# Sparse attention with a gated MLP: DRAM layout of w_in and strided keys, early buffers in w_out's room, and a planner with new DMA and SBUF-port models and newly searched keys

## The chip, the cores and the metric

One core of a Trainium2 chip runs the whole kernel. The metric is the device time of one execution in microseconds; the time before is the median of three runs. Engines: PE (TensorE, matmuls), DVE (VectorE), ACT (ScalarE), POOL (GpSimd), SP (SyncE, which here issues every DMA, in order, on one queue).

## The reference

Eight batches, eight heads, 576 positions, head size 64. Heads 0 to 3 attend to the last 32 positions, heads 4 to 7 to earlier positions of the same residue modulo 32. The result goes through a gated MLP with a spatial mix.

```python
scores = q @ k.T / 8            # masked: local band (h < 4) or strided (h >= 4)
attn = softmax(scores) @ v      # per head; x = heads side by side, (8, 576, 512)
h = relu(x @ w_in)              # w_in (512, 1024), float64
u, v = h[..., :512], h[..., 512:]
v_n = (v - mean(v)) / sqrt(var(v) + 1e-6)
v_s = w_spatial @ v_n + b_spatial          # over the 576 positions
out = (u * v_s) @ w_out         # w_out (512, 512), float64
```

## The kernel before, in words

The work is float32 on a PE that multiplies a rounded form, so each operand is split in a rounded part and a rest (`rnd`, L368, and `rest`, L382), and each product takes three matmuls (PROD, L65). A *unit* t is one batch and a pair of heads; units 0, 1 of a batch are local, 2, 3 strided (NHP = 4 a batch). A unit loads q, k and v, makes scores on PE (L468 local, L611 strided), softmax on DVE and ACT, transposes on DVE (L549, L665), spreads the transposed blocks by rounding copies (L378 on POOL, L376 on ACT), multiplies with v (L578, L681) and writes x, its rounded part by ACT (L398) and its rest by DVE (L386).

A batch then goes through `moe_1` (v tiles, L916: x by w_in's second half, with relu, mean and variance, `chain`, L870; then u, L958), `moe_tail` (the last 64 positions) and `moe_2` (spatial mix, L1038 with the tail's L1050 and L1051; gate, L1060; then the product with w_out by a scheme of seven block products, L1127, sums L1155, stores L1148).

The weights w_in and w_out are float64 in DRAM and are decoded on the core: for each block of 128 rows by 512 columns `words` (L732) loads 512 KB, ACT rescales the high word (L748), POOL or DVE takes three bits of the low word (L757), DVE merges them (L765); then `rnd` and `rest` split it. The first four blocks of w_in land in the vn buffer, the next in u and g buffers. w_out's blocks are combined (L784) and split into w_out_sb (L333).

Buffers are rings (`Ring`, `Buf`, L109 to L136): q, k and raw v have two each, and the third user waits for the first's readers. Unit 2's v lies in the xt buffer instead (L707). The strided keys go to two fixed halves of kbd (L339), by the parity of t, cleared once (L1249).

The order is not written out by hand. Every step is added to `Program` (L139) with a key (its priority), its choice of engines with a cost for each, and what it reads and writes. `order` (L177) plays a list schedule through: the engine that is free first takes the ready step with the lowest key, or hands it to another engine on which it would end sooner; the issue order of each engine is what comes out, and the chip then runs these fixed queues. KEYS (L40) holds the numbers: due keys `a` of the first eight units, keys of the weight blocks (`v`, `u`, `s`, `t`, `o`) and of their loads (`lv`, `lu`, `ls`, `lo`), fillers, and the offsets `p` and `b` of the product steps. The steps of batch 0 and later have keys from 0 to some 400, so a key below 0 goes ahead of them and one in the thousands behind. `dp` is a penalty on DVE: 4195 ns for steps that do not lock the port with POOL, -23103 ns (a preference) for those that do. A load is modelled by its bytes at 310 GB/s (L64, L405) with 2000 ns until others see it (L78). A step of DVE or POOL that uses the shared SBUF port waits in the model until the other's is over (`begin`, L194). `fillers` (L288) puts idle matmuls (L1308) into modelled gaps of PE.

Of the kernel before, what the change touches and what calls it, by code (L numbers as in the profile page):

```python
# [19 lines left out]
DM = H * D  # L20
DFF = 1024
HF = DFF // 2
P = 128
# [20 lines left out]
    "s": (10.2, 4874.8, -256.8, 6409.8,),  # L44
    "t": (-1208.4,),
    "o": (4940, 2540.1, 5013.1, -12547.9,),
    "cst": (-12548.1,),
    "lead": (-0.71,),
    "fill": (1087.1, -65.1, -84.5, -3603.9, -724.5, -3137.8,),
    "dp": (4195.2, -23103.3,),  # L50
    "dpt": (865.03,),
    "lv": (-1100.4, -14982.5, -8252.6, 965.3,),
    "lu": (-391.5, -714.9, 584.7, -450.2,),
    "lo": (-4609.9, -1286.9, 727, -106.8,),
    "ls": (3914.1, 2245.4, 3737.9, 8661.3, 3210,),
    "near": (1768.91,),
    "p": (8.97, 17.05, 0.39,),
    "b": (-3.32, -3.82, 4.52, -4.56, 6.06, 24.46, 13.81, 15.33, 0.17, -3.06, 18.98,),
# [5 lines left out]
DMA_RATE = 310.0  # L64
# [13 lines left out]
    DMA: dict.fromkeys(ENGINES, 2000.0),  # L78
# [20 lines left out]
class Fixed:  # L99
# [39 lines left out]
class Program:  # L139
# [3 lines left out]
    def __init__(self):  # L143
        self.ops, self.writer, self.readers, self.spare = [], {}, {}, {}
        self.tiled, self.port = {}, {}

    def add(self, key, choices, fn, reads=(), writes=(), spare=None, tiled=0, port=()):


        n = len(self.ops)  # L150
        if port:
            self.port[n] = port
        if spare is not None:
            self.spare[n] = spare
# [12 lines left out]
        for tok in (*reads, *writes):
            buf = tok[0]
            if isinstance(buf, Buf):
                deps.update(buf.before)  # L170
                if buf.n > buf.ring.bufs:
                    deps.update(buf.last.users[:1])
                buf.users.append(n)
        deps.discard(n)
        self.ops.append((key, choices, fn, deps))

    def order(self):  # L177
# [7 lines left out]
        free = dict.fromkeys(ENGINES, 0.0)  # L185
        wait = {e: [] for e in ENGINES}
# [4 lines left out]
        held_by = {DVE: (0.0, 0.0), POOL: (0.0, 0.0)}  # L191
# [23 lines left out]
        while len(issued) < len(ops):  # L215
# [39 lines left out]
            if e == PE:  # L255
# [4 lines left out]
            now = begin(n, e, max(free[e], ready_at[n][e]))  # L260
            locks = POOL in self.port.get(n, ())
            held = KEYS["dp"][locks] if now < KEYS["dpt"][0] * 1000.0 else 0.0
            other = [
                (begin(n, o, max(free[o] + queue(o, n), ready_at[n][o])) + c + held * (o == DVE), o)
                for o, c in ops[n][1]
                if o != e
            ]
            if other and min(other)[0] < now + cost + held * (e == DVE):
# [49 lines left out]
def attention_moe(ctx, tc, qT, kT, vl, vs, cst, eye, w_in, w_out, wsp, wtail, out):  # L318
# [14 lines left out]
    w_out_sb = sb.tile([P, len(BLOCKS), 2, 2, DM // 2], F32R, name="w_out_sb")  # L333
# [10 lines left out]

    r_q = Ring(sb, "q", [P, SP], F32, 2)
# [22 lines left out]
    def rnd(key, n, dst, src, reads, writes, engs=(ACT, DVE, POOL), blocks=False):  # L368

        cost = {ACT: 110 + 0.87 * n, DVE: 70 + 0.52 * n, POOL: 110 + 1.75 * n}  # L370
        if blocks:
            cost = {ACT: 200 + 0.85 * n, DVE: 175 + 0.5 * n, POOL: 175 + 0.9 * n}

        def fn(eng):
            if hasattr(eng, "activation"):
                eng.copy(dst(), src())  # L376
            else:
                eng.tensor_scalar(dst(), src(), 1.0, 0.0, op0=ALU.mult, op1=ALU.add)  # L378

        add(key, [(e, cost[e]) for e in engs], fn, reads, writes, port=(DVE,))  # L380
# [23 lines left out]
    def load(key, dst, src, writes, nbytes, reads=()):  # L404
        add(key, [(DMA, nbytes / DMA_RATE)], lambda eng: eng.dma_start(dst(), src), reads, writes)  # L405
# [10 lines left out]
    def normalise(key, st, m, n, p, dst, reads, writes):  # L416
# [12 lines left out]
            key, [(DVE, 70 + 1.04 * n * width), (POOL, 110 + 1.75 * n * width)],  # L429
# [163 lines left out]
    def strided_attention(t, due, q, k, v, vin, kin):  # L593
# [30 lines left out]
        if not masked:  # L624
# [16 lines left out]
            [(DVE, 70 + 1.04 * w)] + ([] if masked else [(POOL, 110 + 1.75 * w)]),  # L641
# [90 lines left out]
    def words(key, fetch, src, n, stage):  # L732
# [19 lines left out]
        def lowest(eng):  # L752
# [7 lines left out]
            key, [(DVE, 70 + 0.52 * n), (POOL, 110 + 1.8 * n)], lowest,  # L760
            [], [low], port=(DVE,),
# [11 lines left out]
    def parts(key, n, val, dst, reads, tok):  # L773
        rnd(key, n, lambda: dst(0), val, reads, [(*tok, 0)])
# [13 lines left out]
    def weight_blocks(kk, bufs):  # L788
# [21 lines left out]
        for b, (name, val, reads) in enumerate((  # L810
# [3 lines left out]
            parts(key, n, val, lambda j, b=b: w_out_sb[:, b, j, kk], reads, ("w_out", name, kk))  # L814
# [55 lines left out]
    def chain(key, v_ps, m, tok):  # L870
# [20 lines left out]
            key, [(POOL, 525)],  # L891
# [129 lines left out]
    def moe_2(b, key):  # L1021
# [98 lines left out]
        def product(block, name, o_ps, a, key, first):  # L1120
            buf, at = place[name]
            b_at = BLOCKS.index(block)
            for kk in range(2):

                def fn(eng, kk=kk):
                    for i, (w, j) in enumerate(PROD):
                        eng.matmul(  # L1127
                            o_ps()[:, :HS],
                            w_out_sb[:, b_at, w, kk, a * P : (a + 1) * P],
# [9 lines left out]
                     *(("w_out", block, kk, w) for w in range(2))],  # L1139
# [85 lines left out]
    add(KEYS["cst"][0], [(DMA, 330)], lambda eng: eng.dma_start(cst_sb, cst), (), [("cst",)])  # L1225
# [91 lines left out]
def _layout(q, k, v, w_in, w_spatial, b_spatial, w_out):  # L1317
# [11 lines left out]
    qT, kT = heads(q, SP, 0), heads(k, STRIDE + S, STRIDE)  # L1329
    vpad = np.zeros((nb, H // 2, S + 32, D), np.float32)  # L1330
# [17 lines left out]
    def words(w):  # L1348
# [11 lines left out]
        "kT": kT,  # L1360
# [4 lines left out]
        "w_in": words(w_in),  # L1365
# [25 lines left out]
```

## Time and profile before

| | |
|---|---|
| median of three runs | 522.7 us (522.42 to 523.24) |
| the profiled execution | 521.19 us |
| its span, first to last instruction | 519.2 us |
| granted PE clock over the span | 0.99 |
| moved by DMA | 52.65 MB, mean 101 GB/s |

The profile gives for each engine the time it was busy, by line and operation, what ended the idle time before it, and the chain of work that ended last. A busy PE is not a useful PE: matmuls overlap, and fillers count. Busy shares over the whole span are an average over a start that loads and decodes, a long even middle and an end, so windows of time are read one by one. SP is no computing engine: its rows are DMA issues, and a gap between two is a wait in its queue.

### The profile page before, as it was taken

How to read it: one execution, taken by the hardware profiler on the slowest of the kernel's cores; microseconds unless marked ns; L12 is line 12 of the kernel's file. 1: busy time of each engine (PE TensorE's matmuls, PEld its weight loads, DVE VectorE, ACT ScalarE, POOL GpSimd, SP SyncE). 2: the span in 40 equal slices, each digit the busy share in tenths (PEclk: the TensorE clock that was granted, in tenths of full speed). 3: DMA queues.
4: the chain of work that ended last, by engine and by line, in shares of the span. 5: the costliest groups of instructions: out<-in, count | busy, mean ns of one | idle time of the engine just before them, and what ended most of it. 6: DMA issues, size and time to landing. Idle time of an engine off the chain costs nothing.

```text
span 519.2 us, 14653 instructions
## 1 busy us (share of the span) xinstructions
PE 502.4 (97%) x5892; PEld 457.8 (88%) x5892; DVE 366.9 (71%) x1101; ACT 264.3 (51%) x809; POOL 125.0 (24%) x253
## 2 busy tenths in 40 slices
PE   7889899999999999999999999999999999999997
PEld 4568799889899899988998899998999899998996
DVE  2899999888597847967389655986469651776166
ACT  6768654678462576417645645534755342223221
POOL 3563542153230213202122212302204010101000
PEclk9799999999999999999999999999999999999999
DMA  7986433653033322252222502232112300020002
GB/s 242 323 293 217 144 135 107 200 179 107 31 115 123 108 73 67 102 156 80 72 95 84 176 1 79 88 122 75 41 55 64 111 0 2 2 89 4 1 1 91
DMA packets 26243, 52.65 MB, mean 101 GB/s; under 512 B 3136, under 2 KB 11584, under 8 KB 26176
## 3 DMA queue, kind: packets, MB, share of 16 engines
q1 hardware_dynamic: 26176, 51.72, 30.5%
q8 instruction: 46, 0.75, 0.6%
q14 instruction: 21, 0.17, 0.1%
HBM read 42.27 MB, written 9.44 MB: 100 GB/s over the span
## 4 chain that ended last, share of the span: by engine, by line
PE 71%; DVE 18%; ACT 4%; DMA 2%; POOL 2%; issue 2%; SPq 1%; DVEq 0%; POOLq 0%; ACTq 0%
PE m L958 18%; PE m L916 16%; PE m L1038 14%; PE m L1127 10%; DVE vn L386 3%; PE po L681 3%; PE po L578 3%; PE s L468 2%; DVE u L784 2%; PE s L611 1%; DVE g L386 1%; DVE u L1060 1%; PE m L1050 1%; PE m L1051 1%; DMA k<-kT 1%
## 5 line engine op out<-in xcount | busy, mean ns | idle before, releaser
L1038 PE MATMUL m<-wsp_sb,vn 128*128 128x288 f32 x768 | 113.5, 299 | 1.6 <-DVE wsp_sb L386 1.6
L1038 PEld LDWEIGHTS m<-wsp_sb,vn 128*128 128x128 f32 x768 | 106.8, 191 | 2.5 <-DVE wsp_sb L386 1.8
L958 PE MATMUL m<-x,w_in_sb 128*128 128x288 f32 x768 | 105.9, 297 | 0.0
L958 PEld LDWEIGHTS m<-x,w_in_sb 128*128 128x128 f32 x768 | 103.4, 188 | 1.4
L916 PE MATMUL m<-w_in_sb,x 128*128 128x512 f32 (+1 forms) x408 | 100.0, 398 | 0.4 <-DVE w_in_sb L386 0.2
L916 PEld LDWEIGHTS m<-w_in_sb,x 128*128 128x128 f32 (+1 forms) x408 | 74.0, 185 | 19.9 <-DVE x L386 0.9
L378 POOL TENSOR_SCALAR ptl<-pc 32x320 f32<-32x320 f32 (+3 forms) x104 | 40.3, 388 | 90.1 <-ACT x L398 32.3
L1127 PE MATMUL m<-g,w_out_sb 128*128 128x288 f32 x384 | 56.8, 299 | 0.2 <-ACT vv L398 0.2
L892 POOL TENSOR_TENSOR bn<-bn,sel 128x1 f32<-128x1 f32 (+1 forms) x37 | 21.4, 581 | 141.4 <-DVE bn L887 141.0
L386 DVE TENSOR_TENSOR x<-po,x 128x288 fp32r<-128x288 f32 x64 | 28.0, 450 | 37.3 <-ACT x L398 36.5
L1127 PEld LDWEIGHTS m<-g,w_out_sb 128*128 128x128 f32 x384 | 52.6, 188 | 1.1 <-ACT vv L398 0.4
L525 ACT ACTIVATE pl<-pl,ml 128x64 f32<-128x64 f32 (+1 forms) x140 | 46.9, 338 | 3.1 <-DVE ml L505 3.0
L874 ACT ACTIVATE vv<-m 128x512 f32<-128x512 f32 (+1 forms) x37 | 22.0, 594 | 47.6 <-PE m L916 41.2
L1127 PE MATMUL m<-vn,w_out_sb 128*128 128x288 f32 x288 | 44.0, 300 | 2.1 <-DVE vn L386 1.4
L1060 DVE TENSOR_TENSOR u<-m,u 128x288 f32<-128x288 f32 x64 | 28.0, 452 | 23.3 <-PE m L1051 22.9
L879 DVE BATCH_NORM_STATS2 bn<-vv 128x6 f32<-128x512 f32 (+1 forms) x37 | 25.4, 687 | 25.5 <-ACT vv L874 25.2
L1127 PEld LDWEIGHTS m<-vn,w_out_sb 128*128 128x128 f32 x288 | 39.6, 188 | 4.3 <-DVE vn L386 2.2
L398 ACT CAST x<-po 128x288 fp32r<-128x288 f32 x64 | 24.7, 398 | 36.0 <-PE po L578 24.3
L972 ACT ACTIVATE u<-m 128x288 f32<-128x288 f32 x64 | 25.9, 409 | 28.4 <-PE m L958 28.2
L376 ACT CAST g<-u 128x288 fp32r<-128x288 f32 x54 | 22.4, 432 | 27.1 <-DVE u L1060 20.6
L376 ACT COPY ptl<-pc 32x320 f32<-32x320 f32 (+3 forms) x88 | 31.4, 357 | 5.9 <-DVE pc L549 4.0
L899 DVE TENSOR_SCALAR vv<-vv,bn 128x512 f32<-128x512 f32 (+1 forms) x37 | 20.6, 557 | 19.3 <-POOL bn L892 19.1
(123 smaller groups left out, 726.5 us busy)
## 6 DMA issues: line engine op xcount, KB each, us to landing
q<-qT SPq DMA_DIRECT2D x32, 295.0 KB, 4.8
v_raw<-vs SPq DMA_DIRECT2D x15, 512.0 KB, 3.8
outT<-o SPq DMA_DIRECT2D x48, 144.0 KB, 1.9
v_raw<-vl SPq DMA_DIRECT2D x16, 384.0 KB, 3.4
k<-kT SPq DMA_DIRECT2D x16, 304.0 KB, 4.5
kbd<-kT SPq DMA_DIRECT2D x32, 144.0 KB, 4.2
outT<-vv SPq DMA_DIRECT2D x16, 144.0 KB, 3.1
vn<-w_in SPq DMA_DIRECT2D x4, 512.0 KB, 6.7
```

What stands on the lines that cost most here:

```text
L376: eng.copy(dst(), src())
L378: eng.tensor_scalar(dst(), src(), 1.0, 0.0, op0=ALU.mult, op1=ALU.add)
L386: eng.tensor_tensor(dst(), src(), f32(hi()), op=ALU.subtract)
L398: eng.copy(dst(), src())
L525: eng.activation(p_sb()[:m, u, :], src, AF.Exp, bias=st()[:m, u : u + 1], scale=SCALE if masked else -1.0, **total,)
L879: lambda eng: eng.bn_stats(bn()[:m, 0:6], v()[:m]), [(v,)], [(bn,)],
L916: eng.matmul(v_ps()[:m, :], x_at(kt)[:, a, :], w_in_sb[:, w, kt, HF:], start=(n == 0 and i == 0), stop=(n == NT - 1 and i == 2),)
L958: eng.matmul(u_ps()[:, :HS], w_in_sb[:, w, kt, f * P : (f + 1) * P], xs[NHP * b + kt]()[:, a, r], start=(n == 0 and i == 0), stop=(n == NT ...
L972: lambda eng, u=u, f=f, u_ps=u_ps: eng.activation(u()[:, f * HS : (f + 1) * HS], u_ps()[:, :HS], AF.Relu),
L1038: eng.matmul(s_ps()[:, :HS], vn()[:, a, kt, fs], wsp_sb[:, w, kt, r], start=(kt == 0 and i == 0), stop=False,)
L1060: lambda eng, ug=ug, s_ps=s_ps: eng.tensor_tensor(ug(), s_ps()[:, :HS], ug(), op=ALU.mult),
L1127: eng.matmul(o_ps()[:, :HS], w_out_sb[:, b_at, w, kk, a * P : (a + 1) * P], at(j, kk), start=first and kk == 0 and i == 0, stop=kk == 1 an ...
```

## The change

- **DRAM layouts.** The host stores w_in as blocks, so that a block's 128 rows of 512 columns lie in one run, and the strided heads' keys as `ks`, one run for each of the two loads of a unit.
- **Homes.** w_out_sb becomes the second user of a ring with one buffer; its first user, `room`, holds q of units 2 and 3 and v of unit 3 (`Part`). Unit 6's v joins unit 2's in xt. w_out's blocks are given keys no earlier than the dues of units 0 to 3, and wait for the readers of the room.
- **Planner: transfers.** A load occupies the queue for 470 ns, transfers stream one behind the other at 370 GB/s after a lag of 1500 ns, and are seen 500 ns after their last byte. ACT starts after a table load of 1280 ns.
- **Planner: port.** Two steps on the shared port run at the same time, each stretched by a share (`SLOWED`), and the stretch is handed on to those that wait.
- **Planner: costs.** New POOL costs for rounding, two-input steps (200 + 2.0n ns), the bit step and the power.
- **Keys.** All of KEYS is new, with `dp` at 12894.8 and -1038.4.

The arithmetic and the number of steps stay as they are.

```diff
 KEYS = {
-    "a": (-1571.4, -4625.4, -1560.3, -729.5, 1426.5, 1095.5, 1503.9, 1519,),
-    "v": (3216.4, -1871.4, 2555.7, -7289.2,),
-    "u": (3205.1, 9316, 1081.3, -773.8,),
+    "a": (-7906.0, -7964.0, -15830.5, -4267.6, 1379.5, 702.2, 2039.1, -3334.8,),
+    "v": (5971.0, -3908.5, -3534.4, 726.2,),
+    "u": (4329.4, -8322.8, -3410.6, -6121.6,),
...
-    "o": (4940, 2540.1, 5013.1, -12547.9,),
-    "cst": (-12548.1,),
+    "o": (1519.5, 3986.0, -8051.8, 12581.5,),
+    "cst": (-11921.6,),
...
-    "dp": (4195.2, -23103.3,),
+    "dp": (12894.8, -1038.4,),
...
-    "lv": (-1100.4, -14982.5, -8252.6, 965.3,),
-    "lu": (-391.5, -714.9, 584.7, -450.2,),
+    "lv": (-2858.0, -4582.1, -8989.4, -1041.3,),
+    "lu": (66.6, -1740.1, -5229.0, 1297.1,),
...
-    "p": (8.97, 17.05, 0.39,),
-    "b": (-3.32, -3.82, 4.52, -4.56, 6.06, 24.46, 13.81, 15.33, 0.17, -3.06, 18.98,),
+    "p": (2.79, 10.51, 0.21,),
+    "b": (25.62, -1.03, 29.44, -12.2, 10.78, 11.69, 33.63, 25.64, -64.18, 15.47, 14.89,),
 }
-DMA_RATE = 310.0
+SLOWED = ((0.3, 0.15), (0.45, 0.6), (0.9, 0.8))
+DMA_RATE, DMA_ISSUE, DMA_LAG, DMA_TAIL, TABLE_LOAD = 370.0, 470.0, 1500.0, 500.0, 1280.0
...
-        def begin(n, e, at):
+        def shared(n, e, at, cost):
             if e in self.port.get(n, ()):
-                since, until = held_by[peer[e]]
+                since, until, share, _ = held_by[peer[e]]
                 if since <= at < until:
-                    return until
-            return at
+                    both = min(until - at, cost)
+                    slow = SLOWED[max(share, self.share[n])]
+                    return (slow[0] * both, slow[1] * both) if e == DVE else (slow[1] * both, slow[0] * both)
+            return 0.0, 0.0
...
+            if e == DMA:
+                moved = max(moved, now + DMA_LAG) + self.bytes[n] / DMA_RATE
+                free[e] = max(now + DMA_ISSUE, moved - DMA_LAG)
+                end = moved + DMA_TAIL
...
-    w_out_sb = sb.tile([P, len(BLOCKS), 2, 2, DM // 2], F32R, name="w_out_sb")
+    r_wo = Ring(sb, "w_out_sb", [P, len(BLOCKS), 2, 2, DM // 2], F32R, 1)
+    room, w_out_sb = r_wo.new(), r_wo.new()
...
+    early_q = [part(NU * D + i * SP, SP) for i in range(2)]
+    early_v = Part(room, lambda t: part(0, NU * D).view(t).rearrange("p (u d) -> p u d", d=D))
...
-        cost = {ACT: 110 + 0.87 * n, DVE: 70 + 0.52 * n, POOL: 110 + 1.75 * n}
+        cost = {ACT: 110 + 0.87 * n, DVE: 70 + 0.52 * n, POOL: 200 + (1.65 if apart else 1.0) * n}
...
-        cost = {DVE: 70 + 1.04 * n + extra, POOL: 120 + 2.3 * n}
+        cost = {DVE: 70 + 1.04 * n + extra, POOL: 200 + 2.0 * n}
...
-        q, k = r_q.new(), None
-        if t == 2:
+        q, k = early_q[t - 2] if t in (2, 3) else r_q.new(), None
+        if t == 3:
+            v = place = early_v
+        elif t in (2, 6):
             place = r_xt.new()
...
-                    kT[b, hp, j::2, STRIDE:], [("k", t % 2, j)], 64 * S * 4, [("k0", t % 2)],
+                    ks[b, hp - 2, j], [("k", t % 2, j)], 64 * S * 4, [("k0", t % 2)],
...
-                    KEYS[name][i], KEYS["l" + name][i], w_in[rows, cols], HF,
+                    KEYS[name][i], KEYS["l" + name][i], w_in[i, c], HF,
...
-                max(KEYS["o"][kk], jobs[-1][0]) + 0.01 * kk,
+                max(KEYS["o"][kk], jobs[-1][0], *(due(t) for t in range(NHP))) + 0.01 * kk,
```

More of the change, by code (lines that the diff above doesn't have):

```diff
@@ L185, in order @@
         free = dict.fromkeys(ENGINES, 0.0)
+        free[ACT], moved = TABLE_LOAD, 0.0
         wait = {e: [] for e in ENGINES}
@@ L259, in order @@
                 cost += FETCH_COST * max(0.0, -stock)
-            now = begin(n, e, max(free[e], ready_at[n][e]))
-            locks = POOL in self.port.get(n, ())
+            now = max(free[e], ready_at[n][e])
+            locks = POOL in self.port.get(n, ()) and self.share[n] == 1
             held = KEYS["dp"][locks] if now < KEYS["dpt"][0] * 1000.0 else 0.0
[L263 to L268, printed above, removed]
+            other = []
+            for o, c in ops[n][1]:
+                if o != e:
+                    at = max(free[o] + queue(o, n), ready_at[n][o])
+                    other.append((at + c + shared(n, o, at, c)[0] + held * (o == DVE), o))
+            if other and min(other)[0] < now + cost + shared(n, e, now, cost)[0] + held * (e == DVE):
                 e = min(other)[1]
                 cost = dict(ops[n][1])[e]
-                now = begin(n, e, max(free[e], ready_at[n][e]))
+                now = max(free[e], ready_at[n][e])
             taken[n] = True
             if e in self.port.get(n, ()):
-                held_by[e] = (now, now + cost)
-            free[e] = now + cost
+                more, theirs = shared(n, e, now, cost)
+                cost += more
+                p = peer[e]
+                begun, until, share, m = held_by[p]
+                if theirs and free[p] == until:
+                    free[p] = until = until + theirs
+                    held_by[p] = (begun, until, share, m)
+                    for j in after[m]:
+                        for o in ENGINES:
+                            ready_at[j][o] = max(ready_at[j][o], until + LAT[p][o])
+                held_by[e] = (now, now + cost, self.share[n], n)
+            free[e] = end = now + cost
+            if e == DMA:
+                moved = max(moved, now + DMA_LAG) + self.bytes[n] / DMA_RATE
+                free[e] = max(now + DMA_ISSUE, moved - DMA_LAG)
+                end = moved + DMA_TAIL
             issued.append((now, n, e))
@@ L278, in order @@
                 for o in ENGINES:
-                    lag = LAT[e][o]
-                    ready_at[m][o] = max(ready_at[m][o], now + cost + lag)
+                    ready_at[m][o] = max(ready_at[m][o], end + LAT[e][o])
                 left[m] -= 1
@@ L317, in attention_moe @@
 @with_exitstack
-def attention_moe(ctx, tc, qT, kT, vl, vs, cst, eye, w_in, w_out, wsp, wtail, out):
+def attention_moe(ctx, tc, qT, kT, ks, vl, vs, cst, eye, w_in, w_out, wsp, wtail, out):
     nc = tc.nc
@@ L378, in fn @@
                 eng.tensor_scalar(dst(), src(), 1.0, 0.0, op0=ALU.mult, op1=ALU.add)
-        add(key, [(e, cost[e]) for e in engs], fn, reads, writes, port=(DVE,))
+        add(key, [(e, cost[e]) for e in engs], fn, reads, writes, port=(DVE, POOL), share=0)
     def rest(key, n, dst, src, hi, reads, writes, engs=(DVE, POOL), extra=0):
-        cost = {DVE: 70 + 1.04 * n + extra, POOL: 120 + 2.3 * n}
+        cost = {DVE: 70 + 1.04 * n + extra, POOL: 200 + 2.0 * n}
         def fn(eng):
@@ L759, in words @@
         add(
-            key, [(DVE, 70 + 0.52 * n), (POOL, 110 + 1.8 * n)], lowest,
-            [], [low], port=(DVE,),
+            key, [(DVE, 70 + 0.52 * n), (POOL, 190 + 1.07 * n)], lowest,
+            [], [low], port=(DVE, POOL), share=2,
         )
@@ L1138, in product @@
                     [*((buf, name, kk, j) for j in range(2)),
-                     *(("w_out", block, kk, w) for w in range(2))],
+                     *((w_out_sb, block, kk, w) for w in range(2))],
                     [(o_ps,)],
```

72 lines of the change are left out of this document (43 added, 29 removed).

## The prediction

> **What bounds the kernel now.** I read the page first, then the busy time by stage, then the timelines of TensorE (PE) and SyncE (SP) through the start, and last the chain at the end.
>
> ```profile
> span 519.2 us, 14653 instructions
> PE 502.4 (97%) x5892; PEld 457.8 (88%) x5892; DVE 366.9 (71%) x1101; ACT 264.3 (51%) x809; POOL 125.0 (24%) x253
> ...
> 5.00:10.00 5.00, 3.61 (x61) 2.29 (x62) 1.99 (x3) 3.26 (x8) 1.32 (x2) 1.00 1.01 383
> 10.00:15.00 5.00, 1.75 (x115) 1.34 (x108) 2.78 (x7) 2.18 (x11) 0.00 (x0) 0.73 0.56 161
> 15.00:20.00 5.00, 4.49 (x75) 2.60 (x76) 4.74 (x14) 3.96 (x15) 1.64 (x4) 0.59 0.99 355
> 20.00:40.00 20.00, 17.39 (x290) 12.40 (x288) 18.11 (x35) 14.38 (x31) 13.67 (x22) 1.00 0.86 301
> 40.00:60.00 20.00, 19.92 (x203) 17.79 (x205) 18.62 (x75) 18.71 (x67) 10.89 (x20) 1.00 0.61 205
> 60.00:72.00 12.00, 9.83 (x130) 9.22 (x127) 11.94 (x26) 5.03 (x13) 4.55 (x8) 0.86 0.53 182
> 72.00:90.00 18.00, 17.68 (x203) 16.72 (x201) 17.67 (x49) 9.48 (x26) 5.27 (x9) 1.00 0.19 60
> 90.00:500.00 410.00, 408.03 (x4720) 378.50 (x4719) 278.40 (x867) 199.19 (x627) 82.39 (x176) 1.00 0.25 80
> 500.00:520.00 20.00, 15.67 (x116) 15.20 (x114) 12.58 (x30) 3.85 (x11) 1.58 (x3) 1.00 0.17 60
> ```
>
> The columns of a stage are its length, then the busy time of PE, weight loads, VectorE (DVE), ScalarE (ACT) and GpSimd (POOL), the granted clock, the DMA share and GB/s. From 90 to 500 us PE is busy 408.0 of 410 us and DVE only 278.4: there the kernel is PE's, no other engine can shorten it, and the change takes no matmul away. What can be won lies before 90 us, and a little after 500. Before 90 us DVE is the full engine: 18.1 of 20, 18.6 of 20, 11.9 of 12 and 17.7 of 18 us from 20 on. But from 5 to 15 us it is busy only 4.8 of 10 us, and the DMA engines drop to a share of 0.56 between 10 and 15: the data came late. PE's own rows tell how late its work starts.
>
> ```profile
> 9.57 0.96 PE L468 MATMUL m<-k,q 64*32 64x64 f32 x72 [1.39 <-DMA k<-kT]
> ...
> 15.51 1.19 PE L611 MATMUL m<-kbd,q 128*32 128x36 f32 x64 [2.38 <-DMA kbd<-kT]
> 16.45 4.48 PE L1308 MATMUL po<-zeros 128*32 128x256 f32 x14
> 20.86 1.21 PE L578 MATMUL po<-ptl,v_raw 128*64 128x96 f32 x24
> 22.95 1.84 PE L916 MATMUL m<-w_in_sb,x 128*128 128x512 f32 x6
> ...
> 40.08 2.83 PE L916 MATMUL m<-w_in_sb,x 128*128 128x512 f32 x11 [0.21 <-DVE w_in_sb L386]
> 42.75 3.36 PE L958 MATMUL m<-x,w_in_sb 128*128 128x288 f32 x24
> ...
> 63.29 7.21 PE L1038 MATMUL m<-wsp_sb,vn 128*128 128x288 f32 x41 [1.55 <-DVE wsp_sb L386]
> ```
>
> L1308 are fillers, so "busy" there is no work; the first matmul with w_in is at 22.95 us, the last v tile (L916) of batch 0 runs at 40.08, released by the last decoded w_in block. Later there is a hole of 1.55 us, ended by DVE. SyncE shows why the data came late.
>
> ```profile
> 5.31 0.33 SPq L405 DMA_DIRECT2D k<-kT  x1
> 10.57 0.33 SPq L405 DMA_DIRECT2D q<-qT  x1
> ...
> 17.46 0.44 SPq L405 DMA_DIRECT2D vn<-w_in  x1
> 22.12 0.33 SPq L405 DMA_DIRECT2D v_raw<-vs  x1
> ...
> 22.96 0.91 SPq L405 DMA_DIRECT2D vn<-w_in  x2
> ...
> SPq L405 <- DMA q<-qT: 3.0, 1, 3.0
> SPq L405 <- PE m L468: 1.9, 1, 1.9
> ...
> SPq L405 <- PE po L578: 4.1, 1, 4.1
> ...
> DMA to landing us min/median/max: 6.2/6.9/7.6
> ```
>
> Two stalls of the one load queue: 5.64 to 10.57 us, 3.0 + 1.9 us, until the first unit's scores (L468) free a q buffer; and 17.90 to 22.12, 4.1 us, until its value product (L578) frees a v buffer. Everything behind waits. The last row is of the two w_in loads of 22.96: the second, issued at about 23.4, lands 7.6 us later, at 31.0.
>
> **The change part by part.** *Homes in w_out's room.* Units 2 and 3 get their q, and unit 3 its v, in a place that nobody holds, so both stalls above lose their cause. The w_out blocks must then wait until those are read; in the trace their splitting starts after 53 us (row below), over 10 us after the last v tile needs unit 3, so this new wait costs nothing; if w_out were moved ahead of 40 us it would cost what it comes early. What the first stall is worth: up to and including that w_in load at 23.4 us SyncE issued 8 w_in blocks (524 KB each), units 1, 0 and 2 and 3 (1.0, 1.0, 1.12 and 1.12 MB by their tile sizes; unit 0's v among them) and constants of 0.16 MB, 8.6 MB. At the 355 GB/s of the full row 15:20 that is 24.2 us, and 31.0 - 24.2 puts the start of a stream without holes at 6.8. The share of 0.56 between 10 and 15 is worth 2.2 us of hole, and the second stall none that shows (0.99 in 15:20). So the same loads without the first stall end at about 28.8.
>
> *Order of the loads.* By the new keys unit 2 is first (due -15830, its loads 34 to 20 earlier), then constants, w_in v2, units 1 and 0, then u2, v1, unit 3, and only then v0, u1, v3; u0, u3 and units 5, 4, 6 have positive keys and come last. So the last v block, v3, has 7.56 MB up to it, not 8.6: 21.3 us, and from the same start of 6.8 - 2.2 = 4.6 it lands at 25.9; with unit 7 ahead of it (1.12 MB more) at 29.0. Data is earlier by 2 to 5 us. The price: before, two w_in blocks were decoded in DVE's idle time of 6 to 11 us (part of its 4.8 us of work there); now DVE has only unit 2 then, whose q and keys land after 1.3 MB, 3.7 us after 4.6, at about 8.3, against 15.5 for its scores before, while unit 1 comes some 0.5 us later than its 9.57. DVE had 5.2 us idle between 5 and 15; I let it use 3 of them. Everything up to 90 us is DVE's queue, so 3 us earlier in its first 15 us is 3 us earlier at 40 and at 90, where PE takes over. Ends: 0 (DVE fills nothing) and 5.2 (all of it). I take 3.0, near the 2 to 5 us of the data.
>
> *DRAM runs.* w_in's rows were runs of 4 KB at an 8 KB pitch, and become one run of 512 KB; strided keys likewise, with runs of 2.3 KB at double pitch.
>
> ```profile
> 27.90:31.00 3.10, 2.46 (x38) 2.15 (x39) 2.49 (x7) 1.77 (x5) 2.80 (x5) 1.00 0.97 328
> 31.00:34.40 3.40, 3.24 (x14) 2.14 (x12) 3.40 (x6) 1.92 (x5) 0.73 (x2) 1.00 0.98 353
> 5.80:7.80 2.00, 2.00 (x14) 1.38 (x13) 0.69 (x1) 0.69 (x4) 0.33 (x1) 1.00 0.98 363
> ```
>
> By the order of issue the first of these stretches moves w_in only, the second whole-run q, k and v: 328 against 353 GB/s. But the third is mostly w_in too and has 363. By the first pair the 4.2 MB of w_in save 12.8 - 11.9 = 0.9 us of DMA; by the third nothing. I take 0.2 of end time, as DVE is the bound behind it.
>
> *New costs and the SBUF port in the planner.* No arithmetic changes, only order and engine. Before, the penalty -23103 kept every two-input step that both DVE and POOL can do on DVE; now it is -1038, so with over 1 us queued on DVE some go to POOL (the diff's 200 + 2.0n, 776 ns for 288 columns), and single-input rounding is priced lower on POOL. What that costs on the full DVE is seen here, first DVE, then POOL:
>
> ```profile
> 54.27 0.89 DVE L784 TENSOR_TENSOR g<-g,g 128x256 f32<-128x256 f32 x1
> ...
> 77.27 0.41 DVE L784 TENSOR_TENSOR g<-g,g 128x256 f32<-128x256 f32 x1
> ...
> 53.65 0.42 POOL L378 TENSOR_SCALAR w_out_sb<-g 128x256 fp32r<-128x256 f32 x1
> ...
> 54.85 1.98 POOL L378 TENSOR_SCALAR w_out_sb<-g 128x256 fp32r<-128x256 f32 x3
> ```
>
> The same step takes 0.41 us alone and 0.89 beside POOL; POOL's takes 0.42 and 0.66. A step of 0.41 to 0.45 us moved from DVE to POOL thus gives DVE 0.45 and costs it up to 0.48 if a two-input step of DVE meets it, nothing if DVE is then on PSUM or a reduction. Per moved step that is -0.45 to +0.03; with about ten such steps before 90 us, 4.5 us won to 0.3 lost. I take 0.3 won, near the bad end, since DVE's queue there is full of two-input steps (L386, L784).
> The Trainium skill (SBUF — State Buffer, "Who interferes with whom") calls the port pair an exclusive lock that the loser waits out in full. The 0.89 fits that as well as sharing; what the lock would make of this change is the last rival.
>
> *The body and the end.* From 90 to 500 us a new order can win at most 410 - 408.0 = 2.0 us; DVE's 278 of 410 us leaves it room, so I take 0, with ends of -0.5 and +1.5. At the end the chain leaves PE for DVE:
>
> ```profile
> 504.07 0.15 PE m L1051
> ...
> 510.37 5.47 PE m L1127 x39
> ...
> 515.87 0.46 DVE o L1155
> ```
>
> 504.2 to 510.4 us is DVE's, the last store another 3 us. The new keys (products at 10.51 instead of 17.05, splits of b11 at +25.62 instead of -3.32) reorder just this stretch, without less work in it. From the 6.1 us PE works through part; I take 0, ends -1.5 and +1.5.
>
> Sum: -3.0 - 0.2 - 0.3 = -3.5 us. The profiled execution took 521.2 us (span 519.2 and 2.0 around it), so it would be 517.7; the median of the three times is 522.7, 1.5 above it, so the forecast is **519.2 us**.
>
> **The rivals.** *All starts fall into place*: DVE uses its whole 5.2 us, the hole at 61.7 us (1.55 us) closes because the spatial weights come sooner, and the clock of 0.86 in 60:72 that follows it rises (0.14 of 12 us, 1.7). With half of the last two that is 5.2 + 1.6 = 6.8: about 516. For it: both stalls have their cause removed. Against: a wholly new order must also not lose elsewhere.
> *DVE's work decides alone*: its busy time is 29.7 us up to 42 us (the sum over the rows), the same steps must run, unit chains leave DVE waiting for exp on ACT and for splits, and earlier data only waits longer. Gain 0 to 0.8: about 522.5.
>
> ```profile
> 0.00:42.00 42.00, 33.22 (x541) 22.02 (x542) 29.69 (x79) 29.83 (x76) 20.32 (x39) 0.92 0.83 284
> ```
>
> Against it: 12.3 us of idle DVE in that row, most before 15.
> *The stall moves to unit 7 (slower).* Its q, keys and v have keys of -3369 to -3355, ahead of w_in v0, u1 and v3 (-2858 to -1041). Its v needs the v buffer that unit 1's value product frees (20.86 + 1.21 in the rows). That product now stands behind unit 2 on DVE, some 2.9 us of its steps. If SyncE reaches that load first, it stands till about 25; after its stall at 10.57 the scores of unit 2 started 4.9 us later (15.51) for 0.6 MB (1.7 us), so a restart costs 3.2 us; unit 7's v (1.5 us) and v0, u1 and v3 (1.57 MB, 4.4 us) land at 34.1, 3.1 us later than 31.0. The blocks u2 and v1, decoded by then, give back about 1 of that: 2 us slower, 524.7. It decides from the point where that product ends after 23. Against: the planner puts a load only where its buffer is free by its own times.
> *The lock (slower).* If POOL's two-input steps hold DVE for their whole length, fifteen of them of 0.78 us before 90 us cost up to 11.7 us and give 15 x 0.45 = 6.8; with a gain of 3.2 at the start the end is +1.7, about 524.4. It decides from ten steps or so. The skill's rule is the one named above; the 0.89 row alone can't refuse it.
>
> **How the numbers follow.** Forecast 0.46, all in place 0.17, DVE alone 0.15, unit 7 0.12, the lock 0.10. About 0.2% (1.0 us) is what this measurement tells from no change, so faster means under 521.7: 0.46 + 0.17 = 0.63; same 0.15; slower 0.12 + 0.10 = 0.22. The forecast's own range is 517.0 to 521.5 (its unknown ends at the start of 0 and 5.2). For 8 in 10 it reaches down to 515.5, which leaves out a third of the best case, and up to 524.3, which leaves out over half of the two slow ones: 0.06 + 0.13.
>
> **What would show it.** Right: SyncE has no stall of 4 us before 15 us, DMA share near 1 from 5 to 20, PE's first scores are L611 before 9.6 us, the first L916 is several us before 22.95, the last v tile of batch 0 at about 37 instead of 40.08, and 90 us' worth of work is reached about 3.5 us sooner; the body keeps under 0.5% of idle PE. Wrong: DVE gaps of the same size before 15 us, a new SyncE wait on L578 before v3's load, POOL two-input steps beside DVE steps of 0.9 us, new PE gaps after 90 us, or a longer stretch from the last L1051 to the end than the 15.1 us of now (504.1 to 519.2).

## The result, and the profile after

The changed kernel takes **519.36 us** (median of four runs, 518.85 to 519.78), the kernel before 522.56 (521.89 to 523.24) on the same chip: a ratio of 0.9938, 95% interval 0.9921 to 0.9955. The forecast was 519.2. The total came out; most of the steps to it did not, as the two traces show.

The page of the kernel after, first line, busy times, and the chain that ended last:

```profile
span 517.7 us, 14663 instructions
...
PE 499.6 (97%) x5884; PEld 459.3 (89%) x5884; DVE 363.0 (70%) x1093; ACT 267.4 (52%) x825; POOL 129.0 (25%) x245
...
PE 89%; DVE 4%; DMA 2%; ACT 2%; SPq 1%; POOL 1%; issue 1%; POOLq 0%
```

Of the chain, 89% is PE; before it was 71%, with 18% DVE. The profiled executions took 519.78 (after) and 521.19 us (before), spans 517.7 and 519.2. The spans lie 1.5 us apart, the medians 3.2: before's profiled time is 1.4 below its median, after's is the slowest of its four. So these two traces can explain 1.5 us. The other 1.7 is in executions that nobody traced.

Busy time by stage, after (columns as in the prediction):

```profile
5.00:10.00 5.00, 3.22 (x79) 2.21 (x77) 1.09 (x3) 2.29 (x6) 0.64 (x1) 1.00 0.94 301
10.00:15.00 5.00, 2.46 (x131) 2.03 (x132) 3.39 (x12) 1.38 (x6) 0.00 (x0) 0.57 0.99 370
15.00:20.00 5.00, 3.61 (x27) 1.63 (x28) 3.51 (x9) 3.79 (x15) 2.15 (x4) 0.50 1.03 408
20.00:40.00 20.00, 16.64 (x271) 13.20 (x270) 18.99 (x37) 15.83 (x40) 10.10 (x19) 0.89 0.85 298
...
60.00:72.00 12.00, 7.72 (x34) 6.34 (x33) 11.42 (x35) 9.65 (x33) 9.40 (x10) 0.72 0.25 87
...
90.00:500.00 410.00, 409.96 (x4661) 382.60 (x4660) 276.36 (x875) 201.41 (x639) 78.61 (x166) 1.00 0.25 79
```

The DMA hole of 10 to 15 us is filled (share 0.99, before 0.56), and yet DVE is busy 8.0 us from 5 to 20, less than the 9.5 of before. The data came early and DVE did not use it. PE's clock is worse: 0.57, 0.50 and 0.89 in the rows from 10 to 40, before 0.73, 0.59 and 1.00. And the body shows almost nothing idle: 0.04 of 410 us, before 1.97.

PE's timeline of the start, after:

```profile
8.79 0.76 PE L650 MATMUL m<-kbd,w_out_sb 128*32 128x36 f32 x64 [1.12 <-DMA kbd<-ks]
...
21.99 2.36 PE L957 MATMUL m<-w_in_sb,x 128*128 128x512 f32 x9
...
41.38 3.06 PE L957 MATMUL m<-w_in_sb,x 128*128 128x512 f32 x12
44.28 2.96 PE L999 MATMUL m<-x,w_in_sb 128*128 128x288 f32 x21
...
67.21 8.65 PE L1079 MATMUL m<-wsp_sb,vn 128*128 128x288 f32 x47 [4.28 <-DVE wsp_sb L422]
```

The strided scores (L611 of before, now L650) come at 8.79 instead of 15.51. The lead melts: the first matmul with w_in is 1.0 us earlier than before (21.99 to 22.95), the last v tiles 1.3 later (41.38 to 40.08), u 1.5 later (44.28 to 42.75), and the hole before the spatial mix has grown from 1.55 to 4.28.

**Where the time went, by a count that overlaps can't blur.** A 288-column matmul shows 0.30 us busy, but undisturbed the next one starts 0.133 us later; the first fence of the body below has ten in 1.49 us. I counted each matmul at its undisturbed interval (512 columns 0.233, 288 columns 0.133, the small ones of attention 0.012 to 0.049, fillers 0; 479.7 us in all) and call the rest of the elapsed time lost. The intervals are those at full clock, so what half clock adds is counted as lost too:

| lost, us, up to | 20 | 30 | 40 | 60 | 70 | 80 | 100 | 140 | 500 |
|---|---|---|---|---|---|---|---|---|---|
| before | 16.3 | 19.3 | 21.5 | 22.1 | 25.4 | 26.3 | 27.7 | 28.6 | 35.7 |
| after | 16.2 | 17.6 | 22.6 | 23.5 | 29.1 | 30.2 | 30.6 | 31.3 | 34.5 |

The start, to 100 us, is 2.8 us *worse*. The body from 100 to 500 loses 4.0 instead of 8.0: 4.0 us better. What is left after 500 is 0.4 better. -4.0 - 0.4 + 2.8 = -1.6, the difference of the spans.

The body, before, around one of its waits:

```profile
276.92 1.49 PE L1127 MATMUL m<-vn,w_out_sb 128*128 128x288 f32 x10
279.02 1.20 PE L1127 MATMUL m<-vn,w_out_sb 128*128 128x288 f32 x7 [0.60 <-DVE vn L386]
```

Ten matmuls of 0.133 us from 276.92 put the next start at 278.25; it comes at 279.02, and is 0.1 us slow itself: 0.87 us are lost, where the row shows 0.60 idle. A wait under 0.16 us does not show at all, it is covered by the drawn length of the matmul before it. The waits of the weight loads, which aren't stretched like that, show more of it. 140 to 500 us, before, then after:

```profile
PEld m L1127 <- DVE vn L386: 2.1, 3, 0.8
...
PEld m L1127 <- DVE o L1155: 1.2, 3, 0.4
```

```profile
PEld m L1168 <- ACT vv L434: 0.3, 1, 0.3
```

Before, the product with w_out (L1127, now L1168) waited six times for a split rest (L386) or a sum (L1155) of DVE. With two more waits of about 0.1 us, too short for this view, eight lost 3.7 us by my count; after, the product stage loses 0.5.

### The profile page after: what moved, and what is told of

Same layout as the page of the kernel before. It is cut to its first block, busy times and chain, and to the rows that moved or that the text cites. A ratio compares the mean times of both kernels' runs of the same rounds, so it can differ in the third digit from the quotient of the medians.

```text
span 517.7 us, 14663 instructions
## 1 busy us (share of the span) xinstructions
PE 499.6 (97%) x5884; PEld 459.3 (89%) x5884; DVE 363.0 (70%) x1093; ACT 267.4 (52%) x825; POOL 129.0 (25%) x245
## 4 chain that ended last, share of the span: by engine, by line
PE 89%; DVE 4%; DMA 2%; ACT 2%; SPq 1%; POOL 1%; issue 1%; POOLq 0%
PE m L1079 20%; PE m L957 18%; PE m L1168 18%; PE m L999 18%; PE po L720 4%; PE po L617 3%; PE s L507 3%; PE s L650 2%; PE m L1091 2%; PE m L1092 2%; DMA k<-kT 1%; SPq L442 1%; DMA x<-wsp 1%; PE po L1349 1%; DVE w_in_sb L422 0%
## 5 line engine op out<-in xcount | busy, mean ns | idle before, releaser
L957 PE MATMUL m<-w_in_sb,x 128*128 128x512 f32 (+1 forms) x408 | 99.5, 399 | 0.0
L1168 PE MATMUL m<-g,w_out_sb 128*128 128x288 f32 x384 | 56.9, 298 | 0.0
L414 POOL TENSOR_SCALAR ptl<-pc 32x64 f32<-32x64 f32 (+3 forms) x89 | 37.9, 426 | 64.7 <-DVE pc L588 24.2
L1168 PEld LDWEIGHTS m<-g,w_out_sb 128*128 128x128 f32 x384 | 52.3, 188 | 1.0 <-ACT vv L434 0.3
L422 DVE TENSOR_TENSOR x<-po,x 128x288 fp32r<-128x288 f32 x64 | 27.6, 447 | 36.3 <-ACT x L434 35.6
L1101 DVE TENSOR_TENSOR u<-m,u 128x288 f32<-128x288 f32 x64 | 28.1, 453 | 30.9 <-PE m L1092 30.7
L412 ACT CAST g<-u 128x288 fp32r<-128x288 f32 x46 | 19.2, 434 | 50.2 <-DVE u L1101 49.0
L1168 PE MATMUL m<-vn,w_out_sb 128*128 128x288 f32 x288 | 42.6, 297 | 0.0
L920 DVE BATCH_NORM_STATS2 bn<-vv 128x6 f32<-128x512 f32 (+1 forms) x37 | 25.3, 683 | 21.0 <-ACT vv L915 20.5
L1168 PEld LDWEIGHTS m<-vn,w_out_sb 128*128 128x128 f32 x288 | 39.5, 188 | 0.4
L412 ACT COPY ptl<-pc 32x64 f32<-32x64 f32 (+3 forms) x103 | 35.7, 346 | 4.7 <-DVE pc L588 2.6
L422 DVE TENSOR_TENSOR g<-u,g 128x288 fp32r<-128x288 f32 x64 | 27.0, 449 | 7.9 <-ACT g L412 6.2
```

Source lines behind the costliest of these rows:

```text
L422: eng.tensor_tensor(dst(), src(), f32(hi()), op=ALU.subtract)
L920: lambda eng: eng.bn_stats(bn()[:m, 0:6], v()[:m]), [(v,)], [(bn,)],
L957: eng.matmul(v_ps()[:m, :], x_at(kt)[:, a, :], w_in_sb[:, w, kt, HF:], start=(n == 0 and i == 0), stop=(n == NT - 1 and i == 2),)
L1101: lambda eng, ug=ug, s_ps=s_ps: eng.tensor_tensor(ug(), s_ps()[:, :HS], ug(), op=ALU.mult),
L1168: eng.matmul(o_ps()[:, :HS], w_out_sb()[:, b_at, w, kk, a * P : (a + 1) * P], at(j, kk), start=first and kk == 0 and i == 0, stop=kk == 1 ...
```

## The experiments

Two questions were open. *The body*: did the new offsets p and b alone end the product's waits, or did the planner with its port model, or only both? *The start*: why did filling the load queue win nothing? Theories: the data still bounds it, at the next stall (D); DVE's work in its new order bounds it, whatever the data does (E); the half clock holds it back (I); DVE's queue is full, and what is pulled forward makes something else late (L). A side question was whether two-input steps on POOL hold DVE up.

All kernels were timed beside runs of before on the same chip. The chips differ between rows (before took 521.9 us beside layout_old, pb_old, pb_new and keys_old, 522.6 and 522.7 beside the others), so rows are best compared by their ratios. "Lost" is of the profiled execution, counted as above. Those single executions lie up to some 3 us from the median of their kernel, so I use them for where, and the medians for how much. As a gauge: "layout_old" has the same order as after, and its losses agree with after's within 0.25 us at every mark of the table.

| kernel | median us | ratio to before, 95% | profiled us | lost to 100 | lost 140 to 500 |
|---|---|---|---|---|---|
| before | 522.56 | 1 | 521.19 | 27.7 | 7.1 |
| after | 519.36 | 0.9921 to 0.9955 | 519.78 | 30.6 | 3.2 |
| layout_old | 518.77 | 0.9930 to 0.9954 | 519.72 | 30.4 | 3.4 |
| pb_old | 521.97 | 0.9993 to 1.0015 | 523.00 | 31.6 | 5.2 |
| pb_new (on before) | 521.67 | 0.9984 to 1.0015 | 521.22 | 28.4 | 6.9 |
| body_keys (on before) | 524.95 | 1.0029 to 1.0059 | 526.13 | 29.5 | 8.2 |
| keys_old | 531.50 | 1.0160 to 1.0205 | 530.57 | 32.9 | 5.5 |
| no_port | 526.73 | 1.0066 to 1.0112 | 524.87 | 31.2 | 7.4 |
| cost_old | 521.55 | 0.9972 to 0.9994 | 521.33 | 31.1 | 4.3 |
| dp_old | 521.96 | 0.9970 to 1.0006 | 518.92 | 28.5 | 3.8 |
| no_homes | 523.70 | 1.0015 to 1.0048 | 526.71 | 36.3 | 4.8 |
| unit7_late | 523.74 | 1.0015 to 1.0046 | 524.11 | 35.0 | 2.7 |
| warm_more | 521.96 | 0.9976 to 1.0011 | 520.45 | 31.5 | 3.2 |
| s_early | 521.59 | 0.9968 to 1.0003 | 520.00 | 30.8 | 3.0 |

**layout_old** is after with the DRAM layouts of before.

```diff
-                    ks[b, hp - 2, j], ...
+                    kT[b, hp, j::2, STRIDE:], ...
...
-                    KEYS[name][i], KEYS["l" + name][i], w_in[i, c], HF,
+                    KEYS[name][i], KEYS["l" + name][i], w_in[rows, cols], HF,
```

> The changed kernel with w_in and the strided keys read as before (4 KB runs at 8 KB pitch; 2.3 KB runs at double pitch); the order is the same, since the planner does not see the layout. If the layout is worth what the 328 against 353 GB/s rows say: start up to 0.9 us later, 519.6 to 520.3. If it is worth nothing: 519.4, and the w_in transfers have the same rate.

518.77 us (518.47 to 519.72), ratio 0.9942 to after's 0.9938: as fast as after. The DRAM runs are worth nothing that shows here.

**pb_old** is after with p and b of before; **pb_new** is before with p and b of after. pb_old's lines, of which pb_new's are the reverse:

```diff
-    "p": (2.79, 10.51, 0.21,),
-    "b": (25.62, -1.03, 29.44, -12.2, 10.78, 11.69, 33.63, 25.64, -64.18, 15.47, 14.89,),
+    "p": (8.97, 17.05, 0.39,),
+    "b": (-3.32, -3.82, 4.52, -4.56, 6.06, 24.46, 13.81, 15.33, 0.17, -3.06, 18.98,),
```

> The changed kernel with only the keys p and b (product stage) put back to those of before. Theory A (the gain lies in the body, where the product stage no longer waits for split pieces, and it comes from the new p and b keys): about 522.5 us, with idle of PE on the product line released by DVE splits back at about 2 us between 90 and 500 us. Theory B (it comes from the planner's new costs, port model and DVE penalty): 519.4, no such waits. Theory C (my prediction: an earlier start): 519.4 too, and the first v tile no later.

> The kernel before with only the keys p and b put to the new ones; old planner, old layouts, no homes. Theory A: about 519 (3 to 4 us faster than before), start up to 60 us as before, product waits gone. Theory B and theory C: 522.6, within 1 us of before.

Both are level with before (521.97 and 521.67). In the new planner the old p and b bring waits of the product stage back, 2.3 us by my count (0.5 in after). The weight loads' waits in pb_old, 140 to 500 us:

```profile
PEld m L1168 <- DVE o L1196: 1.3, 5, 0.3
PEld m L1168 <- DVE vn L422: 0.5, 2, 0.3
```

In the old planner the new p and b change the body's loss by 0.3 us. So they are needed and don't suffice.

**body_keys** is before with all keys that act on the body: p, b, lead, near, dp, dpt. **keys_old** is after with all of KEYS as before.

```diff
-    "lead": (-0.71,),
+    "lead": (-1.3,),
...
-    "dp": (4195.2, -23103.3,),
-    "dpt": (865.03,),
+    "dp": (12894.8, -1038.4,),
+    "dpt": (657.16,),
...
-    "near": (1768.91,),
+    "near": (4868.39,),
...
```

> The kernel before with the keys p, b, lead, near and the DVE penalty of the changed one; planner, layouts and buffers of before. Theory A2 (the gain of the body needs p and b together with lead, near or the penalty): 518 to 520, product waits gone, start as before. Theory B (it needs the planner's new costs): 521 to 523 as with p and b alone.

> The changed kernel (layouts, homes, new planner) with all KEYS of before. Theory A: no gain, 522.5 or slower, product waits present. Theory B: 519 to 520, product waits gone. Theory C: start 3 us earlier than before, 519 to 520.

Old planner and new body keys: 8.2 us lost in the body, 524.95 us in all. New planner and old keys: 5.5 in the body, but 39.9 lost up to 140 us (after 31.3), 531.5 in all. Old planner 6.9 to 8.2, new planner with old p and b 5.2 to 5.5, both new 3.2: the body's gain comes of the pair. The homes go with the new planner in these kernels, and their part isn't separated (no_homes below loses 4.8).

**no_port** sets the stretch of steps that share the port to zero in the planner, and **cost_old** undoes the eight new POOL costs.

```diff
-SLOWED = ((0.3, 0.15), (0.45, 0.6), (0.9, 0.8))
+SLOWED = ((0.0, 0.0), (0.0, 0.0), (0.0, 0.0))
```

```diff
-        cost = {DVE: 70 + 1.04 * n + extra, POOL: 200 + 2.0 * n}
+        cost = {DVE: 70 + 1.04 * n + extra, POOL: 120 + 2.3 * n}
...
-            key, [(POOL, 590)],
+            key, [(POOL, 525)],
```

> The changed kernel with a planner that takes no slowdown on the shared port (SLOWED all zero). If the port model is the part of the planner that helps the body: PE time lost between 140 and 500 us goes from 3.2 back to about 5 us, total 521 to 523. If it is not: body as in the changed kernel.

> The changed kernel with the POOL costs of before in the planner (rounding, two-input steps, bit step, power), all else new. If the POOL costs are the part that helps the body: lost time between 140 and 500 us back to about 5 us. If not: about 3.2 us. The start changes with any new order, so the total may move by 3 us either way.

Without the stretch the body's loss is 7.4 us, as with the old planner, of which waits in the product stage are 4.9. The weight loads' waits in no_port, 140 to 500 us:

```profile
PEld m L1168 <- ACT o L434: 2.1, 3, 1.2
...
PEld m L1168 <- DVE o L1196: 1.5, 4, 0.6
...
PEld m L1168 <- DVE vn L422: 0.5, 2, 0.3
```

They are again waits for rounded parts, sums and rests. That is what one gets if the planner believes DVE and POOL steps over too soon and queues PE's product just behind them; that this is why is argued. Shown is that these keys, planned without the stretch, bring the waits back; keys searched without it were not tried. The old costs lose 1.1 us more in the body than the new, between what the two cases expected, and the whole stays 0.9 us faster than before (ratio 0.9983).

**dp_old** gives the two-input steps back their preference for DVE.

```diff
-    "dp": (12894.8, -1038.4,),
-    "dpt": (657.16,),
+    "dp": (4195.2, -23103.3,),
+    "dpt": (865.03,),
```

> The changed kernel with the two numbers of the DVE penalty put back, so that no two-input step goes to POOL (the changed kernel has 8, all before 90 us: w_out and wsp pieces of 0.9 to 1.7 us). Theory G (the lock: those steps cost DVE more than they give): hole at the first spatial mix shorter than 4.28 us, total 1 to 2 us faster, 517.5 to 518.5. Theory H (they relieve DVE): 519.5 to 521. Body between 90 and 500 us as in the changed kernel by both.

In after eight two-input steps had gone to POOL, all before 90 us. Its groups of them, mean ns behind the comma:

```profile
L422 POOL TENSOR_TENSOR w_out_sb<-g,w_out_sb 128x256 fp32r<-128x256 f32 x4 | 3.6, 899 | 0.2
...
L825 POOL TENSOR_TENSOR g<-g,g 128x256 f32<-128x256 f32 x2 | 1.9, 949 | 0.0
...
L422 POOL TENSOR_TENSOR wsp_sb<-x,wsp_sb 128x576 fp32r<-128x576 f32 x1 | 1.7, 1745 | 0.1
...
L825 POOL TENSOR_TENSOR g<-g 128x256 f32<-128x256 f32 x1 | 1.1, 1067 | 0.0
```

And DVE's timeline where it meets them, then POOL's step that it meets first:

```profile
59.04 1.08 DVE L422 TENSOR_TENSOR w_out_sb<-g,w_out_sb 128x256 fp32r<-128x256 f32 x1
```

```profile
58.80 1.04 POOL L825 TENSOR_TENSOR g<-g,g 128x256 f32<-128x256 f32 x1
```

A DVE step of the size that takes 0.41 us alone takes 1.08 there: 0.67 us more. It starts 0.24 us into the POOL step; waiting out the other 0.80 and then running 0.41 would make 1.21, 0.13 more than measured. By the Trainium skill (SBUF — State Buffer, "Who interferes with whom") a step that finds the port pair taken waits until the other's is over. The 1.08 comes near that, and since POOL's own spans are rough, neither this nor sharing is refuted. With none moved dp_old took 521.96, and its runs spread from 518.92 to 524.33: theory G, which had 517.5 to 518.5, isn't borne out, and H's 519.5 to 521 was missed too. Its profile is of the fastest of them, with a granted clock of 0.990 where the median of its twelve is 0.984, so it says little of the lock. The moved steps cost no total that shows here; whether the lock cost anything stays open.

**no_homes** gives units 2 and 3, and unit 6's v, ring buffers again.

```diff
-        q, k = early_q[t - 2] if t in (2, 3) else r_q.new(), None
-        if t == 3:
-            v = place = early_v
-        elif t in (2, 6):
+        q, k = r_q.new(), None
+        if t == 2:
```

> The changed kernel without the early homes: units 2 and 3 take q from the ring of two, unit 3 and 6 take v from the ring of two. Theory C (homes start the kernel earlier): unit 0's or unit 3's loads wait for unit 2's and unit 1's scores, SyncE stands 4 us or more before 20 us, start 3 us later than in the changed kernel, 522 to 523. Rival F (a stall that is won is given back at the next full ring): start within 1 us, 519 to 520.

523.70 us, 4.3 more than after, and 5.7 more are lost up to 100 us. PE, no_homes:

```profile
44.97 2.60 PE L955 MATMUL m<-w_in_sb,x 128*128 128x512 f32 x10 [0.72 <-DVE x L422]
...
80.23 0.40 PE L1089 MATMUL m<-wt_h,tail 128*128 128x288 f32 x1 [4.26 <-DVE tail L422]
```

With *these* keys the homes are needed: the last v tiles come 3.6 us later than in after, and a hole of 4.26 opens at the tail. This trace is the slowest of its twelve executions. What the homes would do in before's order was not tried; after, with them, has a start that is no better than before's.

**unit7_late** makes unit 7 due late. In after its loads are the new stall. SP, after:

```profile
13.77 0.33 SPq L442 DMA_DIRECT2D q<-qT  x1
16.19 0.33 SPq L442 DMA_DIRECT2D g<-w_in  x1
22.09 1.12 SPq L442 DMA_DIRECT2D kbd<-ks  x2
...
31.45 0.43 SPq L442 DMA_DIRECT2D vn<-w_in  x1
```

```profile
DMA to landing us min/median/max: 6.6/6.6/6.6
```

Unit 7's keys wait from 16.52 to 22.09, 3.3 us for unit 3's keys to land and 2.2 for its scores, and everything behind them too; the last v block, issued at 31.45, lands at 38.0 (the landing row is of it), before at 31.0.

```diff
-    "a": (-7906.0, -7964.0, -15830.5, -4267.6, 1379.5, 702.2, 2039.1, -3334.8,),
+    "a": (-7906.0, -7964.0, -15830.5, -4267.6, 1379.5, 702.2, 2039.1, 2334.8,),
```

> The changed kernel with unit 7's due key at 2334.8 instead of -3334.8, so that its loads come behind w_in v0, u1 and v3. Theory D (in the changed kernel the load queue stands for unit 7's keys until unit 3's scores at 22.06 us, and the last w_in blocks land at 38.0): no SyncE wait of over 4 us between 16 and 23 us, last v block landed by about 30, last v tile of batch 0 at 37 to 39 us instead of 41.38, total 1 to 3 us faster than the changed kernel, 516.5 to 518.5, if the body stays. Rival E (DVE's work decides the start, the load only waits): last v tile stays at 40 to 42, total 519.

523.74 us: slower. Its SP, then its PE:

```profile
19.29 0.43 SPq L442 DMA_DIRECT2D k<-kT  x1
26.31 0.33 SPq L442 DMA_DIRECT2D v_raw<-vl  x1
```

```profile
43.59 2.59 PE L957 MATMUL m<-w_in_sb,x 128*128 128x512 f32 x10 [0.24 <-DVE x L422]
...
80.95 3.25 PE L1079 MATMUL m<-wsp_sb,vn 128*128 128x288 f32 x12 [4.02 <-DVE u L1101]
```

The stall at 16.5 is gone, the last v block lands at 30.9 instead of 38.0, and the next ring stall stands at 19.7 to 26.3 (6.5 us, for a value product). But the last v tiles start at 43.59, 2.2 us *later* than in after, released by DVE's rest of x, and DVE ends a hole of 4.02 later on. In this order seven microseconds of earlier weight data won nothing, so theory D's forecast (37 to 39 for the last v tiles) falls. E has the mechanism, DVE ends these waits, but its numbers (40 to 42, total 519) were missed as well.

**warm_more** lets the planner put more fillers, with the order of the rest unchanged.

```diff
-WARM_END, WARM_GAP, WARM_COST, WARM_COLS, WARM_SHARE = 110000.0, 700.0, 427.0, 256, 0.8
+WARM_END, WARM_GAP, WARM_COST, WARM_COLS, WARM_SHARE = 110000.0, 400.0, 427.0, 256, 1.6
```

> The changed kernel with the same planned order and more idle matmuls ahead of waiting PE steps in the first 110 us (fillers for twice the share of a modelled gap, and for gaps from 400 ns). The changed kernel's profile has PE at half clock for 20.5 us of the first 73 (10.65 to 20.89, 34.55 to 37.96, 65.27 to 72.09), the kernel before for 10.2. Theory I (the half clock holds the start back): fewer half-clock windows before 40 us, 0.5 to 2 us faster, 517.5 to 518.5. Rival J (PE is not the bound there): 519 to 520, or slower as fillers stand ahead of real work.

The half clock shrinks from 20.5 us (after; before 10.2) to 6.8, and the median is 521.96, 2.6 more than after. The fillers themselves push the first scores from 8.79 to 11.87 us, 25.3 instead of 23.2 us are lost by 50, and the hole before the spatial mix is still 3.52. So theory I's forecast falls, as rival J had it (slower, for fillers ahead of real work). But the fillers cost something themselves, so this kernel doesn't show that half clock is free. The traces show that it isn't. PE does the same matmuls in the same order in dp_old as in after up to 47 us, and dp_old has full clock where after has half clock, from 34.55 to 37.96. First dp_old, then after:

```profile
34.56 1.22 PE L720 MATMUL po<-pts,w_out_sb 128*64 128x72 f32 x32 [3.03 <-ACT u L789]
35.72 3.06 PE L957 MATMUL m<-w_in_sb,x 128*128 128x512 f32 x12
...
39.61 3.07 PE L957 MATMUL m<-w_in_sb,x 128*128 128x512 f32 x12
```

```profile
34.97 2.19 PE L720 MATMUL po<-pts,w_out_sb 128*64 128x72 f32 x32 [3.03 <-ACT u L789]
37.09 3.46 PE L957 MATMUL m<-w_in_sb,x 128*128 128x512 f32 x12
```

From here PE waits in neither trace until the last v tiles, which dp_old reaches after 5.05 us and after in 6.41 (at 41.38). These 1.4 us are as much as after's last v tiles come later than before's, and they are the clock. Over all runs it points the same way: within each of the twelve experiments' kernels the executions with less granted clock tend to be the slower ones (correlation -0.27 to -0.87, 0.9 to 3.2 us for each 0.01 of clock).

**s_early** draws the splitting of the spatial weights, which ended after's hole of 4.28 us, forward.

```diff
-    "s": (13308.3, 1709.1, 5210.5, 13961.2,),
-    "t": (2702.5,),
+    "s": (20.1, 20.2, 20.3, 20.4,),
+    "t": (20.5,),
```

> The changed kernel with the spatial weights' processing keys at 20.1 to 20.5, just ahead of the first spatial mix (24.9), instead of thousands, so that their rests no longer stand behind w_out's pieces and unit 6's masks on DVE. Theory K (the hole of 4.28 us at 62.9 us and the half clock after it are time lost): hole under 1 us, total 3 to 5 us faster than the changed kernel, 514.5 to 516.5. Rival L (DVE is full to 90 us, and what goes first makes something else late by as much): hole gone, but new ones before 100 us, 519 to 521.

PE, s_early:

```profile
61.85 6.48 PE L1079 MATMUL m<-wsp_sb,vn 128*128 128x288 f32 x48
...
73.13 0.61 PE L1091 MATMUL m<-wt_h,tail 128*128 128x288 f32 x1 [2.76 <-DVE tail L422]
...
76.64 3.14 PE L1079 MATMUL m<-wsp_sb,vn 128*128 128x288 f32 x12 [1.22 <-DVE u L1101]
```

The hole at 62.6 is gone, and two others of DVE's stand at 70 and 75; 30.8 us are lost by 100, after 30.6. That is theory L, though its total (519 to 521) was missed by 0.6. The median is 521.59, not better than after. The first 48 matmuls of the spatial mix take 6.48 us here at full clock, and 47 take 8.65 in after, at half clock behind its hole: some 2 us of after's loss there is again the clock. No kernel tried here beats after; layout_old equals it.

## Why the prediction was right in sum and wrong in its steps

*The start, forecast -3.0, came out +2.8 in the traces.* The failed step reads "Everything up to 90 us is DVE's queue, so 3 us earlier in its first 15 us is 3 us earlier at 40 and at 90". The first half held: no stall of 4 us before 15, DMA share near 1 from 5 to 20, L650 before 9.6 us. But DVE did not fill its idle time; it was busy 8.0 us from 5 to 20 (9.5 before), and 4.5 of the 10 from 5 to 15 (4.8 before), which the prediction had named as a sign of being wrong. It stood until POOL was done with the first block's low bits, at 7.85, and then three times for PE's scores (1.1, 1.5 and 1.5 us). Nor is everything up to 90 us DVE's queue: ahead of the last v tiles PE waited 3.03 us for ACT, and then worked without a wait at half clock. And an earlier start isn't carried along: what counts is when the last step that PE needs comes. At 67 us that was a step of DVE, later than before. unit7_late and s_early show it: earlier data, or an earlier step, moves the wait elsewhere. The sign given as right, the last v tile at about 37, was wrong (41.38).

*The body, forecast 0, came out -4.0.* The step that failed is "From 90 to 500 us a new order can win at most 410 - 408.0 = 2.0 us". It took the time in which PE is not drawn busy for all that is lost, though its rows overlap. A 288-column matmul is drawn 0.30 us long and costs 0.133, so each wait hides up to 0.16 us, and the real loss was 8.0 from 100 to 500 alone. The Trainium skill (Perfetto Trace Analysis, "Identifying the Most-Contended Engine") says that matmul busy time does not tell how near PE is to its peak. The case agrees: from 90 to 500 us PE is drawn busy 99.5% of the time before and 100% after, and the losses are 4 us apart. The Trainium skill gives as reason that pipelined instructions look smaller in the trace; here they look larger, 0.30 for 0.133.

*The end, forecast 0, came out -0.4.* The chain at the end, after:

```profile
503.02 10.80 PE m L1168 x81
513.82 0.02 issue
513.84 0.46 DVE vv L1196
514.30 0.40 DVE o L1196
```

PE now runs the product without a break to 513.82, where before the chain left it for DVE from 504.2 to 510.4. From the end of the last L1092 (L1051 before) the product takes 10.8 us instead of 11.6, but two sums of DVE stand behind it instead of one, so that the last store comes 0.4 later after it. Of the 6.1 us, 0.4 came out.

*Layout, forecast -0.2*: nothing, by layout_old. *POOL, forecast -0.3*: eight steps moved, not ten; no effect that dp_old could show. *Unit 7's stall* came, though first for its keys (5.6 us, for unit 3's keys and scores) and only then, as that rival described, for its v until unit 1's value product, to 25.99 (the rival: about 25). Its price of 2 us isn't borne out: without the stall the kernel is slower. *DVE's work decides alone* was the rival nearest to the start, and had 0.15; the half clock, which has a part in it, stands in none of the terms of the sum.

So -3.5 was the sum of three terms of which none came true, and the size is met by one I had put at zero: that the total came out was luck. That the median moved 3.2 us and the spans 1.5 is not settled: the executions of before alone spread from 519.9 to 524.0 us on one chip, and a trace holds one each.

One more thing the runs show together: each of the seven changes of planner numbers or keys to after that alter its order cost 2.2 to 12.1 us in the median. This fits keys that suit one model and each other; then taking one part out measures not that part's worth but that of an order no longer searched.

## What to carry to other kernels

Read a pipelined PE by the interval from one matmul to the next, not by its busy share: 0.5% idle went with 8 us lost in 400. Before giving a gain to an earlier load, name the last step that the waiting engine needs and show that it comes earlier too; a full in-order queue in between swallows the lead. If an order was searched with a model, judge the model's terms by the waits that they leave in the trace, and change order and model together.

## What the runs showed of the hardware

Half clock came in stretches of 3.41 and 6.83 us in before and of 3.41, 6.83 and 10.24 in after (10.65 to 20.89), one, two and three times 3.41. A stretch of it made 32 value matmuls take 2.19 us instead of 1.22. The Trainium skill (TensorE: Matmul & The Clock Gate, "Part 1: The HAM clock gate") has windows of about 3.4 us for that; the traces agree. Not expected was that 13.7 us less of it, bought with fillers that delay the first scores by 3.1 us, came out 2.6 us slower. Runs of 4 KB at an 8 KB pitch cost the kernel no more than runs of 512 KB (ratios 0.9942 and 0.9938 to before). Two-input fp32 steps of 128x256 take POOL 0.90 to 1.07 us beside DVE, and a step of DVE that meets one takes 1.08 instead of 0.41.
